# Attention followed by a top-1 mixture of experts: a new order for the last two batches, and evacuations and router steps on other engines

## The chip, the cores and the metric

The kernel runs on one core of a Trainium2 chip. The metric is device time in microseconds of one execution. The profile is one execution recorded by the hardware profiler; its span, from the first to the last instruction, is a little different from the measured times.

The engines have these names in the profile: PE is TensorE (PEld its weight loads), DVE is VectorE, ACT is ScalarE, POOL is GpSimd, SP is SyncE, which here only issues DMAs. Each engine runs its instructions in the order of the program, so an instruction that waits holds up all behind it on the same engine.

## The reference

Eight batches of 448 tokens, 12 heads of 64. Attention with a softmax whose denominator has an extra term, then a router by cosine similarity that picks one of eight experts for each token, and the two-layer expert, scaled by the router's probability.

```python
# q, k, v: (8, 12, 448, 64)
scores = scale * np.matmul(q, k.transpose(0, 1, 3, 2))
m = np.max(scores, axis=-1, keepdims=True)
e = np.exp(scores - m)
attn = e / (np.sum(e, axis=-1, keepdims=True) + np.exp(-m) + 1e-09)
x = np.matmul(attn, v)                      # -> (3584, 768) after the transpose

xn = x / (norm(x) + 1e-06)
en = expert_emb / (norm(expert_emb) + 1e-06)
logits = xn @ en.T / tau
expert_idx = np.argmax(logits, axis=1)
gate_w = softmax(logits)[expert_idx]
for e in range(8):
    mask = expert_idx == e
    h = np.maximum(x[mask] @ w1[e], 0.0)    # w1: (8, 768, 1024)
    out[mask] = gate_w[mask, None] * (h @ w2[e])   # w2: (8, 1024, 768)
```

The kernel computes, for each batch, the expert that most of its tokens chose; other experts follow in a conditional part at the end, which no token needs with these inputs.

## The kernel before

The program is a hand-written schedule. `put(slot, fn)` files a piece of work under a time mark, and at the end all pieces are emitted in the order of their marks. That gives each engine its order; waits between engines follow from the data and from the buffers. A slot has 8 marks (`NSLOT = 8`) and handles one pair of heads (48 pairs, `G`, six for each batch, `NP`). Attention runs through the slots; the expert work of a batch (15 products, `moe_chunks`) is spread over the slots of later pairs, from pair `LAG = 11` after the batch's first. `FILL` says where in each slot: three, three, one, two, three and three products.

```python
LAG = 2 * NP - 1
FILL = 2 * ((2.8, 5.3, 5.4),) + ((2.8,), (2.8, 5.4)) + 2 * ((2.8, 5.3, 5.4),)
```

Attention of one pair. `front_qk` transposes q and k; `scores` makes the scores in four parts (j = 0 to 3), exponentials on ScalarE and the subtraction of one on VectorE (`em`); `attend` multiplies by v in the next slot, takes the reciprocal of the denominator as exp(-ln) on ScalarE, and `normalise` makes x on VectorE. `square` gives the squares for the router's norms.

```python
def attend(k, g, s):
    ...
    def recip():
        nc.scalar.activation(rd[:], ps[:, :, 0:S], ACT.Ln, bias=1.0, scale=1.0 / (S + 1.0))   # L281
        nc.scalar.activation(rd[:], rd[:], ACT.Exp, scale=-1.0)                               # L282
    k.put(s + 0.04, rest)
    k.put(s + 2.3, recip)
```

The router of one batch: matmuls with the expert vectors (`router_mm`, L336) and a copy to SBUF (L342), transposes to token order (`router_tok`, L350), logits, maximum and one-hot (`router_logits`, L358 to L370), a matmul with ones that counts the choices (`router_pick`, L431), maximum and index of the counts (`router_count`), the index into a register (`router_index`), the loads of that expert's weights (`fetch`, L464), and on the side the probabilities (`router_pow`, `router_exp`, `router_act`, `router_gate`).

```python
def router_logits(k, b, tp):
    ...
    nc.vector.reduce_max(out=m[:], in_=l[:], axis=AX.X)
    nc.vector.tensor_tensor(out=l[:], in0=l[:], in1=m[:]..., op=ALU.subtract)      # L366
    nc.vector.tensor_scalar(out=oh[:], in0=l[:], ..., op0=ALU.is_equal)             # L368
    nc.vector.tensor_tensor(out=ohb[:], in0=oh[:], in1=k.mask[:], op=ALU.mult)      # L370

def router_exp(k, b):
    nc.gpsimd.tensor_scalar_add(nrm[:], nrm[:], 1e-6 * (S + 1.0))                   # L382
    nc.gpsimd.tensor_tensor(out=nrm[:], in0=nrm[:], in1=k.less[:], op=ALU.pow)      # L383
    nc.gpsimd.tensor_tensor(out=l[:], in0=l[:], in1=nrm[:]..., op=ALU.mult)         # L384

def router_act(k, b):
    k.nc.scalar.activation(l[:], l[:], ACT.Exp)                                     # L390
```

An expert product fills one PSUM buffer of the pool `work`, which has two, and is then evacuated to SBUF by ScalarE or VectorE, as the flag `vec` says. The pool is shared with the transposes of k, the fourth part of the scores and the router's transposes.

```python
n.work = pool("work", 2, space=PSUM)

def moe_h(k, xb, w1, f, hs, later=now, vec=False):      # 8 of them: first layer, L504
    ps = k.work.tile([128, 512], F32, name="work", tag="work")
    ...
        if vec: nc.vector.tensor_scalar_max(h[:], ps[:, 0:S], 0.0)                  # L512
        else:   nc.scalar.activation(h[:], ps[:, 0:S], ACT.Relu)                    # L514

def moe_y(...)     # 6: second layer, L532, evacuated at L522 (VectorE) or L524 (ScalarE)
def moe_yr(...)    # 1: the remainder of 64 tokens, L551, evacuated the same way
```

And the schedule:

```python
    put(-NSLOT, lambda: warm(k, 18))                      # 18 matmuls that only warm TensorE
    ...
    for b in range(B):
        s = ((b + 1) * NP + 1) * NSLOT
        put(s + 2.85, lambda b=b, s=s: router_mm(k, b, s + 2.75))
        put(s + 7.9, lambda b=b, s=s: router_tok(k, b, s + 7.9))
        s += NSLOT
        put(s + 0.16, lambda b=b: router_pick(k, b))
        put(s + 0.9, lambda b=b: router_pow(k, b))
        put(s + 6.9, lambda b=b: router_count(k, b))
        put(s + 7.05, lambda b=b: router_index(k, b))
        for i, o in enumerate((7.1, 10.5, 14, 20, 26, 32, 38)):
            put(s + o, lambda b=b, i=i: fetch(k, b, i))
        put(s + 7.2, lambda b=b: router_exp(k, b))
        put(s + 10.38, lambda b=b: router_act(k, b))
        ...
    late = {2.8: (4.7, False), 5.3: (7.3, True), 5.4: (8.5, True)}   # evacuation mark, VectorE?
    for b in range(B):
        pos = [((b * NP + LAG + i) * NSLOT, o) for i in range(NP) for o in FILL[i]]
        for (s, o), fn in zip(pos, moe_chunks(k, b), strict=True):
            put(s + o, lambda fn=fn, s=s, l=late[o]: fn(s + l[0], l[1]))
```

Of the kernel before, what the change touches and what calls it, by code (L numbers as in the profile page):

```python
# [23 lines left out]
SM = 384  # L24
# [112 lines left out]
def load_qk(k, n):  # L137

    nc = k.nc
    b, h0 = n // NG, n % NG * 2 * GP  # L140
    s = n % NG
    t = Net()
    t.qm = k.qkp.tile([128, 3, 2 * GP, DH], F32, name="qm", tag="qm")
    t.km = k.qkp.tile([128, 3, 2 * GP, DH], F32, name="km", tag="km")
    t.r, t.v = k.qkrest[s], k.vld[s]

    keng = nc.sync if n else nc.scalar
    for eng, dst, src in ((nc.sync, t.qm, k.q), (keng, t.km, k.k)):
        for j in range(3):
            eng.dma_start(  # L150
                dst[:, j, :, :], src[b, h0 : h0 + 2 * GP, 0:SM, :].rearrange("h (p t) d -> t p h d", t=3)[j]
            )
    for eng, h, src in ((nc.sync, 0, k.q), (keng, 1, k.k)):
        eng.dma_start(t.r[64 * h : 64 * h + 64, :, :], src[b, h0 : h0 + 2 * GP, SM:S, :].rearrange("h p d -> p h d"))
    k.ld[n] = t


# [150 lines left out]
def on_pool(g):  # L308
    return g < LAG - 1 and g % NP < NP - 1
# [14 lines left out]
def square_add(k, g):  # L324
    acc = k.xs[g - g % NP][1]
    k.nc.vector.tensor_tensor(out=acc[:], in0=acc[:], in1=k.xs[g][1][:], op=ALU.add)


def router_mm(k, b, s):

    nc = k.nc
    ps = k.big.tile([128, 512], F32, name="rmm", tag="big")
    for r in range(2):
        for q in range(4):
            x = k.xs[b * NP + 3 * r + q][0] if q < 3 else k.xs[b * NP + (NP - 1) * r][1]
            nc.tensor.matmul(  # L336
                ps[32 * q : 32 * q + 32, 0:S], lhsT=(k.en[:, 3 * r + q, :] if q < 3 else k.ones32[:]), rhs=x[:],
                start=(r == 0), stop=(r == 1),
            )
    for c in range(NP):  # L340
        k.xs.pop(b * NP + c)
    k.put(s + 1.9, lambda: nc.scalar.copy(out=k.rr[:, 0:S], in_=ps[:, 0:S]))  # L342


def router_tok(k, b, s):

    nc, p = k.nc, k.rp
    tp = k.work.tile([128, 4, 128], F32, name="tok", tag="work")
    for t in range(4):
        nc.tensor.transpose(tp[:, t, :], k.rr[:, 128 * t : 128 * t + 128], k.ident[:])  # L350
    k.put(s + 0.12, lambda: router_logits(k, b, tp))


def router_logits(k, b, tp):

    nc, p = k.nc, k.rp
    nrm = p.tile([128, 4], F32, name="nrm", tag="nrm")
    nc.vector.tensor_copy(out=nrm[:], in_=tp[:, :, 96])  # L358
    l = p.tile([128, 4, E], F32, name="l", tag="l")
    nc.vector.reduce_sum(  # L360
        out=l[:], in_=tp[:, :, 0:96].rearrange("p t (q r) -> p t r q", q=3)[:, :, 0:E, :], axis=AX.X
    )
    m = p.tile([128, 4], F32, name="m", tag="m")
    nc.vector.reduce_max(out=m[:], in_=l[:], axis=AX.X)

    nc.vector.tensor_tensor(out=l[:], in0=l[:], in1=m[:].unsqueeze(2).broadcast_to([128, 4, E]), op=ALU.subtract)  # L366
    oh = p.tile([128, 4, E], F32, name="oh", tag="oh")
    nc.vector.tensor_scalar(out=oh[:], in0=l[:], scalar1=0.0, scalar2=None, op0=ALU.is_equal)  # L368
    ohb = p.tile([128, 4, E], BF16, name="ohb", tag="ohb")
    nc.vector.tensor_tensor(out=ohb[:], in0=oh[:], in1=k.mask[:], op=ALU.mult)  # L370
    k.ohb[b], k.lg[b] = ohb, (l, nrm)


# [14 lines left out]
def router_act(k, b):  # L388
    l = k.lg[b]
    k.nc.scalar.activation(l[:], l[:], ACT.Exp)  # L390
# [44 lines left out]
def router_count(k, b):  # L435

    nc, p = k.nc, k.rp
    cnt = k.cnt_all[:, b, :]
    nc.vector.reduce_sum(out=cnt, in_=k.cp.pop(b).rearrange("p (t e) -> p e t", e=E), axis=AX.X)
    mx = p.tile([128, 8], F32, name="mx", tag="mx")  # L440
    k.mx[b] = mx[:, 0:1]
    nc.vector.max(mx[:], cnt)
    nc.vector.max_index(k.idx_all[:, b, :], mx[:], cnt)
    idf = p.tile([128, 1], F32, name="idf", tag="idf")
    nc.vector.tensor_copy(out=idf[:], in_=k.idx_all[:, b, 0:1])
    oh0 = k.oh0_all[:, b, :]
    nc.vector.tensor_scalar(out=oh0, in0=k.iota[:], scalar1=idf[:, 0:1], scalar2=None, op0=ALU.is_equal)


def router_index(k, b):  # L450
# [17 lines left out]
def fetch(k, b, i):  # L468
    w = w_piece(k, k.e0[b], i)
    k.wts[b][i // 3 > 0].append(w)  # L470
# [177 lines left out]
        nc.tensor.matmul(ps[:], lhsT=idb[:, 0:128], rhs=idb.unsqueeze(1).broadcast_to([128, 2, 256]), start=True, stop=True)  # L648


def pipeline(k):

    G = B * NP
# [2 lines left out]
    def put(slot, fn):  # L656
        at.setdefault(round(slot, 3), []).append(fn)
# [24 lines left out]
    for g in range(G):  # L682
        s = g * NSLOT
        put(s - NSLOT + 4.2, lambda g=g, s=s - NSLOT + 4.2: front_qk(k, g, s))
        put(s + 0.8, lambda g=g: front_v(k, g))
        rest = (3, 0.12, 2.3, 2.7) 
        for j, o, pa, pv in ((0, 0, 0.3, 1.5), (1, 0.05, 0.4, 2.6), (2, 5.2, 6, 7.7), rest):
            put(s + o, lambda g=g, j=j, pa=s + pa, pv=s + pv: scores(k, g, j, pa, pv))

        s += NSLOT  # L690
        put(s + 0.1, lambda g=g, s=s: attend(k, g, s + 0.1))
        put(s + 4.75, lambda g=g, s=s: normalise(k, g, s + 4.75))
        put(s + NSLOT + (4.68 if on_pool(g) else 2.35), lambda g=g: square(k, g))
        if 0 < g % NP < NP - 1:
            put(s + 2 * NSLOT + 0.6, lambda g=g: square_add(k, g))
    put(-NSLOT, lambda: warm(k, 18))
    for g in range(LAG):
        for o in (2.8, 5.4):
            put(g * NSLOT + o, lambda: warm(k, 3))
    for b in range(B):  # L700
        s = ((b + 1) * NP + 1) * NSLOT
        put(s + 2.85, lambda b=b, s=s: router_mm(k, b, s + 2.75))
        put(s + 7.9, lambda b=b, s=s: router_tok(k, b, s + 7.9))
        s += NSLOT
        put(s + 0.16, lambda b=b: router_pick(k, b))
        put(s + 0.9, lambda b=b: router_pow(k, b))
        put(s + 6.9, lambda b=b: router_count(k, b))
        put(s + 7.05, lambda b=b: router_index(k, b))
        for i, o in enumerate((7.1, 10.5, 14, 20, 26, 32, 38)):
            put(s + o, lambda b=b, i=i: fetch(k, b, i))  # L710
        put(s + 7.2, lambda b=b: router_exp(k, b))
        put(s + 10.38, lambda b=b: router_act(k, b))
        s += NSLOT
        put(s + 6.95, lambda b=b: keep_rows(k, b))
        put(s + 7.0, lambda b=b: keep_xb(k, b))
        put(s + 6, lambda b=b, s=s: router_gate(k, b, s + 6))

    late = {2.8: (4.7, False), 5.3: (7.3, True), 5.4: (8.5, True)}
    for b in range(B):
        pos = [((b * NP + LAG + i) * NSLOT, o) for i in range(NP) for o in FILL[i]]  # L720
        for (s, o), fn in zip(pos, moe_chunks(k, b), strict=True):
            put(s + o, lambda fn=fn, s=s, l=late[o]: fn(s + l[0], l[1]))
    while at:
        for fn in at.pop(min(at)):
            fn()
# [88 lines left out]
```

## Time and profile before

| | us |
|---|---|
| median of 3 runs | 440.58 (438.2 to 440.62) |
| span of the profiled execution | 444.5 |
| mean granted TensorE clock | 0.965 of full |
| PE, DVE, ACT, POOL busy | 394.7, 326.8, 296.7, 161.8 |
| expert weights, issue to landing | 8.4 (512 KB piece), 6.3 (384 KB piece) |

How to read the profile. Its first part gives the busy time of each engine with its share of the span and the number of instructions. A row of the waits says which engine and line waited for which, then us in total, how many times, and the longest. A row of the timeline gives the start in us, the length, engine, line, operation, what it writes and reads, and in square brackets how long the engine had stood idle before it and what ended that. A row by stretch gives for each engine its busy time in the stretch and the number of its instructions, and at the end the mean granted TensorE clock (1.00 is full), the DMA engines' busy share and the GB/s. Ends of matmuls are modelled, so the busy time of TensorE counts some waiting.

Three stages can be told apart in the busy time of slices: attention alone up to about 84 us, attention with expert work up to about 393 us, and the last router with the rest of the experts to the end.

### The profile page before, as it was taken

Reading aid. Unit: us, or ns where it says so; the run is one execution under the profiler, and the core shown is the slowest. Engines: PE = TensorE matmul, PEld = TensorE weight load, DVE = VectorE, ACT = ScalarE, POOL = GpSimd, SP = SyncE. Lnnn points to the kernel's source line nnn. Section 1 sums busy time; section 2 is a strip of 40 time slices with the busy share of each in tenths; the row PEclk is TensorE's granted clock in tenths of the full one; section 3 lists DMA queues with packets and bytes.
Section 4 is the critical chain, followed back from the end, with each engine's and each line's share of the span. In section 5 each row is a group of like instructions: output and inputs, shape, how many; then the busy total and the mean of one; then the engine's idle time right before and its main releaser. Section 6 shows DMA issues by size and latency. Waiting matters only on the chain.

```text
span 444.5 us, 7234 instructions
## 1 busy us (share of the span) xinstructions
PE 394.7 (89%) x2306; PEld 244.2 (55%) x2306; DVE 326.8 (74%) x787; ACT 296.7 (67%) x442; POOL 161.8 (36%) x237
## 2 busy tenths in 40 slices
PE   6998996999799997999799997999699997998595
PEld 2566554665556565565466564665456564644253
DVE  3789976997778797887788796887778696764122
ACT  1898885869658787688568775869657784842111
POOL 3141337722542138212643137312651218305400
PEclk9899999999999999999899998999989998999789
DMA  9886438983998849993998849993799409914953
GB/s 179 203 193 143 110 79 171 193 172 90 203 227 193 160 86 235 196 216 72 202 206 194 161 92 242 169 201 81 162 223 181 91 1 177 192 41 80 240 91 127
DMA packets 133305, 69.75 MB, mean 157 GB/s; under 512 B 99464, under 2 KB 127112, under 8 KB 133264
## 3 DMA queue, kind: packets, MB, share of 16 engines
q1 hardware_dynamic: 115024, 43.63, 39.5%
q0 software_dynamic: 16384, 25.17, 35.0%
q10 hardware_dynamic: 1856, 0.46, 0.5%
q8 instruction: 19, 0.31, 0.3%
q14 instruction: 22, 0.18, 0.1%
HBM read 83.39 MB, written 16.52 MB: 225 GB/s over the span
## 4 chain that ended last, share of the span: by engine, by line
PE 47%; ACT 19%; DVE 17%; issue 6%; DMA 5%; POOL 5%; SPq 0%; POOLq 0%; ACTq 0%; DVEq 0%
PE work L504 12%; PE work L532 9%; DVE x L295 5%; PE av L273 5%; ACT rd L281 5%; ACT e L240 5%; PE big L229 4%; PE work L235 3%; DVE em L248 3%; PE rmm L336 3%; PE work L551 3%; DMA w<-in_moe_w_dram 2%; DVE qt L200 2%; POOL nrm L383 2%; ACT rd L282 2%
## 5 line engine op out<-in xcount | busy, mean ns | idle before, releaser
L240 ACT ACTIVATE e<-big 128x896 f32<-128x896 f32 x144 | 127.0, 920 | 62.5 <-PE big L229 62.1
L504 PE MATMUL work<-xb,w 128*128 128x448 bf16 x384 | 82.3, 359 | 11.1 <-ACT h L514 5.3
L248 DVE TENSOR_SCALAR em<-e 128x896 fp32r<-128x896 f32 x144 | 86.9, 629 | 2.0 <-ACT e L240 1.5
L295 DVE SCALAR_TENSOR_TENSOR x<-av,rd 64x448 f32<-64x448 f32 x96 | 66.3, 691 | 20.3 <-ACT rd L282 18.4
L532 PE MATMUL work<-w,h 128*128 128x384 bf16 x384 | 73.4, 343 | 2.9 <-ACT y L524 2.1
L273 PE MATMUL av<-em,vab 128*128 128x448 f32 x288 | 67.7, 371 | 0.0
L229 PE MATMUL big<-qt,kt 64*128 64x448 f32 x288 | 58.9, 446 | 5.7 <-ACT kt L196 3.5
L200 DVE CAST qt<-tq 128x448 fp32r<-128x448 f32 x48 | 30.0, 624 | 43.4 <-PE tq L191 43.0
L504 PEld LDWEIGHTS <-w 128*128 128x128 bf16 x384 | 37.5, 103 | 44.0 <-issue 11.8
L273 PEld LDWEIGHTS av<-em,vab 128*128 128x128 f32 x288 | 54.2, 190 | 4.9 <-DVE em L248 0.6
L464 POOL DMA_DIRECT2D w<-in_moe_w_dram x56 | 45.2, 808 | 31.6 <-DVE em L248 20.7
L532 PEld LDWEIGHTS <-h 128*128 128x128 bf16 x384 | 38.6, 104 | 32.9 <-issue 13.2
L178 POOL TENSOR_TENSOR vs<-vs,vld 128x256 f32<-128x256 f32 x48 | 35.3, 736 | 52.3 <-issue 25.9
L281 ACT ACTIVATE rd<-av 128x896 f32<-128x896 f32 x48 | 44.2, 921 | 8.5 <-PE av L278 6.1
L178 POOL TENSOR_TENSOR vs<-vld 128x256 f32<-128x256 f32 x24 | 17.5, 728 | 88.4 <-PE av L278 69.5
L282 ACT ACTIVATE rd<-rd 128x896 f32<-128x896 f32 x48 | 45.7, 952 | 1.5
L229 PEld LDWEIGHTS big<-qt,kt 64*128 64x128 f32 x288 | 24.7, 186 | 34.7 <-issue 9.4
L522 DVE TENSOR_SCALAR y<-work,g 128x384 f32<-128x384 f32 x40 | 24.6, 616 | 24.4 <-PE work L532 14.9
L514 ACT ACTIVATE h<-work 128x448 bf16<-128x448 f32 x32 | 17.1, 534 | 20.2 <-PE work L504 20.2
L512 DVE TENSOR_SCALAR h<-work 128x448 bf16<-128x448 f32 x32 | 19.9, 623 | 13.1 <-PE work L504 12.1
L551 PE MATMUL work<-w,h 128*64 128x384 bf16 x128 | 14.4, 373 | 16.6 <-ACT y L524 16.6
L196 ACT CAST kt<-tk 128x384 fp32r<-128x384 f32 x48 | 22.6, 472 | 9.3 <-PE tk L189 9.2
(105 smaller groups left out, 545.2 us busy)
## 6 DMA issues: line engine op xcount, KB each, us to landing
w<-in_moe_w_dram POOLq DMA_DIRECT2D x24, 512.0 KB, 8.4
w<-in_moe_w_dram POOLq DMA_DIRECT2D x32, 384.0 KB, 6.3
qm<-in_q_dram SPq DMA_DIRECT2D x72, 128.0 KB, 2.9
vld<-in_v_dram SPq DMA_DIRECT2D x24, 384.0 KB, 3.8
out_dram<-y SPq DMA_DIRECT2D x48, 192.0 KB, 6.0
km<-in_k_dram SPq DMA_DIRECT2D x69, 128.0 KB, 4.0
qkrest<-in_q_dram SPq DMA_DIRECT2D x24, 64.0 KB, 4.1
vld<-in_v_dram SPq DMA_DIRECT2D x48, 32.0 KB, 3.8
```

Of the source, the lines that this page charges most:

```text
L178: k.behind(nc.gpsimd.tensor_tensor(out=vs[:], in0=(vs[:] if j > 1 else t.v[:, :, 0, :]), in1=t.v[:, :, j, :], op=ALU.add))
L200: nc.vector.tensor_copy(out=qt[:], in_=pq[:, 0:S])
L229: nc.tensor.matmul(ps[:, h, 0:S], lhsT=kt[64 * h : 64 * h + 64, 128 * j : 128 * j + 128], rhs=qt[64 * h : 64 * h + 64, :], start=True, sto ...
L240: nc.scalar.activation(e[:], ps[:, :, 0:S], ACT.Exp, scale=scale)
L248: k.last = nc.vector.tensor_scalar_sub(em[:], e[:], 1.0)
L273: nc.tensor.matmul(ps[:, h, 0:S], lhsT=va[:, j, h : h + 2, :], rhs=k.ems[g, j][:, h, :], start=False, stop=(j == 2),)
L281: nc.scalar.activation(rd[:], ps[:, :, 0:S], ACT.Ln, bias=1.0, scale=1.0 / (S + 1.0))
L282: nc.scalar.activation(rd[:], rd[:], ACT.Exp, scale=-1.0)
L295: nc.vector.scalar_tensor_tensor(out=x[r, :], in0=ps[r, h, 0:S], scalar=ps[r, 0, S : S + 1], in1=rd[o, h, :], op0=ALU.add, op1=ALU.mult,)
L464: k.nc.gpsimd.dma_start(w[:], src)
L504: nc.tensor.matmul(ps[:, 0:S], lhsT=w1[c // 2][:, c % 2, 128 * f : 128 * f + 128], rhs=xb[:, c, :], start=(c == 0), stop=(c == NP - 1),)
L532: nc.tensor.matmul(ps[:, 0:SM], lhsT=hs[f][:, 128 * t : 128 * t + 128], rhs=w2[f // 2][:, f % 2, SM * n : SM * n + SM], start=(f == 0), st ...
```

## The change

- The first pair of heads of the first batch is loaded alone and ahead of the second, q on SyncE's queue and k on ScalarE's, with the remainders on SyncE's; fewer warming matmuls stand before it (15, not 18).
- Three small steps of the router's one-hot and two steps of the chosen expert's one-hot (now `router_first`, behind the first weight fetch) go from VectorE to GpSimd.
- The router's exponential on ScalarE (`router_act`) and the gates (`router_gate`) come one slot later.
- Evacuations of expert products change engines: the first in a slot goes to VectorE, the second to ScalarE, the last of a two-product slot to ScalarE.
- Batches 6 and 7 have an order of their own (`last_batch`): three products of batch 6 before the last router's matmuls, two between its steps, the other ten of batch 6 and all of batch 7 after it. The last router starts one slot earlier, all its weight fetches are issued close together, the first three ahead of the powers, and the last squares are earlier.

It is meant to take waits off ScalarE and VectorE and to shorten the end, where the last router has little beside it.

```diff
-    keng = nc.sync if n else nc.scalar
-    for eng, dst, src in ((nc.sync, t.qm, k.q), (keng, t.km, k.k)):
-        for j in range(3):
-            eng.dma_start(dst[:, j, :, :], ...)
-    ...
+    if n:
+        ...   # as before, all on nc.sync
+    else:
+        for h in range(0, 2 * GP, 2):
+            for eng, dst, src in ((nc.sync, t.qm, k.q), (nc.scalar, t.km, k.k)):
+                for j in range(2):
+                    eng.dma_start(dst[:, :, h + j, :], src[0, h + j, 0:SM, :].rearrange("(p t) d -> p t d", t=3))
+            for j, src in ((0, k.q), (1, k.k)):
+                nc.sync.dma_start(t.r[64 * j : 64 * j + 64, h : h + 2, :], ...)
 ... (router_logits)
-    nc.vector.tensor_tensor(out=l[:], ..., op=ALU.subtract)
+    nc.gpsimd.tensor_tensor(out=l[:], ..., op=ALU.subtract)
-    nc.vector.tensor_scalar(out=oh[:], ..., op0=ALU.is_equal)
+    nc.gpsimd.tensor_scalar(out=oh[:], ..., op0=ALU.is_equal)
-    nc.vector.tensor_tensor(out=ohb[:], ..., op=ALU.mult)
+    nc.gpsimd.tensor_tensor(out=ohb[:], ..., op=ALU.mult)
 ... (router_count)
-    nc.vector.tensor_copy(out=idf[:], in_=k.idx_all[:, b, 0:1])
-    nc.vector.tensor_scalar(out=oh0, in0=k.iota[:], scalar1=idf[:, 0:1], ..., op0=ALU.is_equal)
+def router_first(k, b):
+    nc.gpsimd.tensor_copy(out=idf[:], in_=k.idx_all[:, b, 0:1])
+    nc.gpsimd.tensor_scalar(out=k.oh0_all[:, b, :], in0=k.iota[:], scalar1=idf[:, 0:1], ..., op0=ALU.is_equal)
 ...
+def last_batch(k, s):                       # s = G * NSLOT
+    b = B - 1
+    at = [s + o for o in (0.5, 1.0, 1.5, 5.5, 6.5)] + [s + 7.5 + 0.5 * i for i in range(25)]
+    out = {0: (s + 0.95, True), 1: (s + 2.5, False), 2: (s + 4.8, True), 3: (s + 5.9, True), 4: (s + 6.6, False)}
+    for i, fn in enumerate(moe_chunks(k, b - 1) + moe_chunks(k, b)):
+        put(at[i], lambda fn=fn, l=out.get(i, (at[i] + 0.45, i % 2 == 1)): fn(*l))
+    put(s + 5.0, lambda: router_mm(k, b, s + 5.2))
+    put(s + 6.0, lambda: router_tok(k, b, s + 6.12))
+    put(s + 7.0, lambda: router_pick(k, b))
+    put(s + 7.1, lambda: router_count(k, b))
+    put(s + 7.2, lambda: router_index(k, b))
+    for i in range(7):
+        put(s + (7.3 if i < 3 else 7.9), lambda i=i: fetch(k, b, i))
+    put(s + 7.4, lambda: router_first(k, b))
+    put(s + 7.5, lambda: router_pow(k, b))
+    put(s + 7.6, lambda: router_exp(k, b))
+    put(s + 9, lambda: router_act(k, b))
+    put(s + 9.1, lambda: router_gate(k, b, s + 9.1))
+    ...
 ... (pipeline)
-        put(s + NSLOT + (4.68 if on_pool(g) else 2.35), lambda g=g: square(k, g))
+        put(s + (4.9 if g == G - 1 else NSLOT + 4.68 if on_pool(g) else NSLOT + 2.35), lambda g=g: square(k, g))
-    put(-NSLOT, lambda: warm(k, 18))
+    put(-NSLOT, lambda: warm(k, 15))
 ...
+        if b == B - 1:
+            last_batch(k, G * NSLOT)
+            break
 ...
+        put(s + 7.15, lambda b=b: router_first(k, b))
         put(s + 7.2, lambda b=b: router_exp(k, b))
-        put(s + 10.38, lambda b=b: router_act(k, b))
         s += NSLOT
         ...
+        s += NSLOT
+        put(s + 2.38, lambda b=b: router_act(k, b))
         put(s + 6, lambda b=b, s=s: router_gate(k, b, s + 6))
-    late = {2.8: (4.7, False), 5.3: (7.3, True), 5.4: (8.5, True)}
-    for b in range(B):
+    late = {2.8: (4.6, True), 5.3: (7.0, False), 5.4: (8.5, True)}
+    for b in range(B - 2):
+        ...   # the second product of a two-product slot: (8.15, False)
```

The marks of the copy after the router's matmuls and of the logits are written in another place but keep their values for the first seven batches.

## The prediction

> **What bounds the kernel now.** I read the page's busy shares first, then the waits of TensorE, then those of ScalarE, then one stalled stretch in order of time, and last the busy time by stretch.
>
> ```profile
> PE 394.7 (89%) x2306; PEld 244.2 (55%) x2306; DVE 326.8 (74%) x787; ACT 296.7 (67%) x442; POOL 161.8 (36%) x237
> ```
>
> TensorE is the fullest engine, and an 89% that holds modelled ends leaves under 50 us of visible gaps. So the first question is who makes these gaps.
>
> ```profile
> PE work L551 <- ACT y L524: 16.6, 6, 3.7
> PE work L504 <- ACT h L514: 5.3, 11, 0.5
> PE work L504 <- DMA w<-in_moe_w_dram: 5.2, 2, 2.9
> PE work L532 <- ACT y L524: 2.1, 6, 0.4
> ```
>
> The columns are us in total, times, longest. Six waits of about 2.8 us, one for each batch whose experts run beside attention, are the largest item: the remainder matmuls (L551) want a PSUM buffer that ScalarE has not emptied (L524).
>
> ```profile
> ACT l L390 <- POOL l L384: 20.1, 8, 3.3
> ```
>
> ScalarE in turn stands in its queue before the router's exponential (L390) until GpSimd has finished the two powers and the product before it. It does so once a batch, 2.5 us on average. The timeline of batch 4's stall shows the three linked:
>
> ```profile
> 265.69 1.31 POOL L383 TENSOR_TENSOR nrm<-nrm,less 128x4 f32<-128x4 f32 x1
> ...
> 267.36 0.23 ACT L390 ACTIVATE l<-l 128x32 f32<-128x32 f32 x1 [2.34 <-POOL l L384]
> 267.50 0.90 ACT L281 ACTIVATE rd<-av 128x896 f32<-128x896 f32 x1
> ...
> 269.28 0.56 ACT L524 ACTIVATE y<-work,g 128x384 f32<-128x384 f32 x1
> ...
> 269.90 1.81 PE L551 MATMUL work<-w,h 128*64 128x384 bf16 x16 [2.79 <-ACT y L524]
> ...
> 271.63 2.74 PE L532 MATMUL work<-w,h 128*128 128x384 bf16 x8
> ```
>
> The power (1.31 us) holds L390; behind L390 stand the logarithm, its exponential and the copy L524; behind L524 stands TensorE. The last line matters as much: eight L532 matmuls take 2.74 us here, while sixteen take 2.76 us elsewhere. The stall also costs clock, as the stretches show (the figure after the brackets of POOL is the granted TensorE clock):
>
> ```profile
> 262.00:267.00 5.00, 5.00 (x32) 3.55 (x32) 4.84 (x16) 2.62 (x4) 2.78 (x3) 1.00 0.89 164
> 267.00:270.00 3.00, 0.21 (x4) 0.21 (x4) 0.98 (x4) 2.61 (x5) 2.47 (x6) 1.00 1.04 205
> 270.00:274.30 4.30, 4.30 (x24) 1.93 (x23) 2.44 (x8) 1.03 (x2) 3.64 (x6) 0.61 1.13 267
> 282.00:290.00 8.00, 7.53 (x46) 4.81 (x43) 6.73 (x15) 6.00 (x9) 2.13 (x3) 1.00 0.81 159
> ```
>
> TensorE idles in 267 to 270, and then works at a mean clock of 0.61 for 4.3 us; in an undisturbed stretch it is at 1.00. The last row also shows the next limits: VectorE is busy 6.73 of 8 us, ScalarE 6.00.
>
> [...] 0.61 after a gap of 2.8 us, and 0.50 for 4.5 us (420.0 to 424.5) after the gap in the tail. [...] the small GpSimd add of L382 takes 0.23 us in the median, but 0.71 us where it starts beside an `em` subtraction on VectorE. This bears on the steps moved to GpSimd. [...] On these 32-element tiles the choice is nearly free: 0.24 us (L384, GpSimd) against 0.19 (L366, VectorE).
>
> **The change part by part.**
>
> *Router exponential one slot later.* It moves eight marks of the schedule on, to where its input has long been there, so the wait is gone and 0.23 us of work stays. To size it I take the times between first attention matmuls (L264) around each of the six stalls: 12.0, 10.3, 12.5, 12.4, 13.4 and 12.4 us, 73.0 in sum. The next slot carries three second-layer products as well; it takes 8.14 us (274.82 to 282.96), 0.34 of it a wait for L524, so 7.8, and the remainder product adds about 0.1. Six times 7.9 is 47.4, so 25.6 us are removed: 16.6 of waits and about 9 of half clock. In batch 0 no expert work runs yet, but the slot from 66.82 to 75.75 takes 8.9 us and the next 7.3, against about 6.4 for its neighbours: some 3 us more. Sum: 28.5 us.
>
> *Evacuations on other engines.* In a slot with three products, the first is now emptied by VectorE instead of ScalarE, the second by ScalarE instead of VectorE. Before, the first stood behind ln and exp on ScalarE, and the second product waited 0.48 us for it (the L504 row above, 5.3 us, and most of the 2.1 us of L532). VectorE sits idle at that moment, waiting for the transposed q (0.96 to 0.99 us in the two slots I looked at), so it can take the 0.62 us copy. It pushes the qt copy and the normalisation back by about 0.1 to 0.5 us; the normalisation ends some 0.9 us before the next attention matmul needs it, so this is just hidden. TensorE's dense work in such a slot is 7.28 us against 7.77 now. VectorE has about 6.6 to 7.3 us of work in the same slot, so I don't count all of it: 5 us of the 7.4.
>
> *Small router steps on GpSimd.* VectorE loses five steps of 0.15 to 0.23 us, about 1 us a batch. But three of them (subtract, compare, mask) lie between the maximum and the counting matmul, which TensorE and the logarithm wait for in order. At present mask ends at 257.74 and that matmul starts at 257.90. On GpSimd the three take about 0.9 us undisturbed instead of 0.7, and VectorE runs copies and subtractions back to back just then[...]. I put the delay at 0.9 us in six batches: minus 5.5 us. The one-hot of the chosen expert moves behind the first fetch, off any path.
>
> *Last two batches.* Before, seven of batch 6's fifteen products run ahead of the last router's matmuls, and these start at 398.63 although their last input is there at 397.3. The slot before also carries three. Now three precede the router. Chain afterwards: the last j = 2 subtraction about 0.6 us earlier, L281 at about 392.4 instead of 393.36, square done at 396.5, last router matmul over at 396.9 instead of 400.4. Then a product is put before the transposes and one before the count (up to 0.7 us lost), GpSimd adds 0.3, so the first weight fetch is issued near 402.8 instead of 405.26. The three first-layer fetches follow at once, instead of at 408.15 and 409.13 with powers between them. The first-layer weights came in spaced 3.2 to 3.5 us (products resumed at 413.7, 416.5, 420.0), so the third should land near 416.5. Twelve products of batch 6, about 15 us, are left to cover this. One new wait: the powers now follow the fetches, so the exponential L390 is ready only near 409.2, and the evacuation of the first second-layer product stands behind it on ScalarE; TensorE loses about 3 us there, with weights still coming. Batch 7 then starts near 417 and needs 18.7 us warm (before: 20 us from 420.02, of which 2.2 were half clock). With the 4.45 us from the last matmul's end to the span's end this gives about 441 against 444.5: 3.5 us.
>
> *First pair alone.* Before, the last piece of k (64 KB, queued behind three pieces on ScalarE's queue, issued at 4.04) held the transposes until 9.19. Now the first pair's pieces, half the bytes, come first. The 15 warming matmuls end near 6.6, and the transposes could start near 7. Later loads share the same full queues (DMA share 1.02 over the first 12 us), so I count 2 us.
>
> Sum: 28.5 + 5 - 5.5 + 3.5 + 2 = 33.5. I take 1 us off for friction, as VectorE comes near to full, and predict 440.6 - 32.5 = 408.
>
> **Rivals.** First, the wait only changes its owner: with slots of 7.3 us VectorE (up to 7.3 us of work) becomes the bound, or the normalisation comes late for the next attention matmul, which already waits for it nine times (3.0 us in total). Against it: the stalled slots have 4.5 us of slack, so only the evacuation gain and a part of the first would go. Time about 416. Second, the counting matmul waits two microseconds or more for GpSimd[...]; then half of the gain of the exponential is given back in the slot before[...]. For it: L409 on GpSimd has a median of 0.56 us against 0.22 at best. Time about 420. Third, DMA becomes the bound: its share is 0.81 to 0.83 of 50 us a batch, which is 0.93 of 44.5 us. Against it: stretches at 1.04 to 1.13 pass without a wait of TensorE for data in the middle. It would add a few us, 412. Fourth, everything overlaps as planned, the count isn't delayed and the tail keeps its clock: 398.
>
> **Range and chances.** 398 to 420 runs from the fourth rival to the second. The 2% mark is 431.8; for it three quarters of the gain would have to be lost, although its largest term is a wait whose cause is taken away outright. Faster by over 2%: 0.95; within 2%: 0.04; slower: 0.01.
>
> **What would show it.** In the profile after: L551 waiting for ScalarE gone, and L390 waiting for GpSimd under 4 us in sum, mostly the tail's; first-attention-matmul spacing of about 7.9 us where it was 12.4; mean clock 0.98 or more. The period of a batch, from one router matmul to the next, falls from 50.3 us to about 45. A new row of the counting matmul or the logarithm waiting for GpSimd's mask, near 5 us. First scores near 8 instead of 10.42. I am wrong if L551's gap is filled by another releaser, if the clock stays at 0.965, or if the tail from the last router's matmuls to the end does not shrink below 44 us (it is 45.9).

## The result, and the profile after

| | before | after |
|---|---|---|
| median, us (4 runs each) | 440.6 (438.2 to 440.84) | 419.1 (416.94 to 420.24) |
| ratio, with 95% interval | | 0.9518 [0.9465, 0.9571] |
| span of the profiled execution, us | 444.5 | 415.3 |
| mean granted TensorE clock | 0.965 | 0.992 |

The change makes the kernel 4.8% faster, 21.5 us. The prediction was 408, with 398 to 420; the result lies at the upper edge of that range. The two profiled spans differ by more, 29.2 us: the execution of the kernel before that was profiled took 446.05 us, well above its median. This will matter below.

The busy shares of the kernel after, from its page:

```profile
PE 384.4 (93%) x2303; PEld 239.6 (58%) x2303; DVE 326.0 (78%) x751; ACT 299.9 (72%) x438; POOL 179.9 (43%) x277
```

TensorE is busy 10.3 us less in all, for the same matmuls but three warming ones: its clock was nearer to full (0.992 in the mean, 0.965 before). VectorE and ScalarE have the work they had, in a shorter span; GpSimd is busy 18 us more. Line numbers shift: L551 is now L562, L524 is L535, L390 is L397, L264 is L271, L281 is L288, L336 is L343. The longest waits of TensorE (us in total, times, longest):

```profile
PE av L271 <- DVE x L302: 6.9, 10, 3.5
PE av L438 <- POOL ohb L377: 6.3, 7, 0.9
PE big L236 <- DVE qt L207: 3.6, 1, 3.6
PE work L562 <- ACT y L535: 2.0, 1, 2.0
```

And the wait of ScalarE that was the target, once 20.1 us in eight times:

```profile
ACT l L397 <- POOL l L391: 4.4, 1, 4.4
```

The six waits of the remainder product beside attention, 16.6 us, are gone. One of 2.0 us is new, in the tail, where the exponential waits for GpSimd; the prediction had about 3 us for it. In their place stands the new wait that the prediction put near 5 us: the counting matmul waits 0.9 us for GpSimd's mask in each of seven batches, 6.3 us in sum. The slot in which batch 4's stall was, and the two after it, by stretch (the figure after the brackets of POOL is the granted clock):

```profile
251.44:259.41 7.97, 7.97 (x57) 5.44 (x58) 7.33 (x19) 6.17 (x9) 5.52 (x9) 1.00 0.96 197
259.41:267.13 7.72, 7.72 (x50) 5.22 (x48) 6.90 (x17) 6.26 (x10) 5.62 (x9) 1.00 1.12 251
267.13:274.39 7.26, 7.26 (x45) 4.63 (x42) 6.62 (x15) 6.11 (x9) 4.01 (x7) 1.00 1.10 203
```

The first row is the 12.4 us slot: now 7.97, with TensorE busy all the time and its clock at 1.00. VectorE is at 7.33 of 7.97 us there.

The steady part repeats to a few hundredths of a microsecond from batch to batch, so a change can be read from the six slots, start to start of the first attention matmul (the columns are worked out from the starts of L264 or L271 in the timelines):

| slot of a batch | before | after |
|---|---|---|
| three first-layer products (two slots) | 7.77 each | 7.23 each |
| one product and the router's matmuls | 7.98 | 7.98 |
| two products and the count | 6.57 | 7.67 |
| two second-layer products and the remainder | 10.3 to 13.4 | 7.97 |
| three second-layer products | 8.14 | 7.72 |

### The profile page after: what moved, and what is told of

It is laid out like the page before. It is cut to its first block, busy times and chain, and to the rows that moved or that the text cites. A ratio compares the mean times of both kernels' runs of the same rounds, so it can differ in the third digit from the quotient of the medians.

```text
span 415.3 us, 7247 instructions
## 1 busy us (share of the span) xinstructions
PE 384.4 (93%) x2303; PEld 239.6 (58%) x2303; DVE 326.0 (78%) x751; ACT 299.9 (72%) x438; POOL 179.9 (43%) x277
## 5 line engine op out<-in xcount | busy, mean ns | idle before, releaser
L255 DVE TENSOR_SCALAR em<-e 128x896 fp32r<-128x896 f32 x144 | 88.5, 640 | 1.3 <-ACT e L247 0.4
L515 PE MATMUL work<-xb,w 128*128 128x448 bf16 x384 | 79.6, 352 | 0.9 <-DMA w<-in_moe_w_dram 0.4
L280 PE MATMUL av<-em,vab 128*128 128x448 f32 x288 | 68.7, 375 | 0.7 <-DVE em L255 0.7
L543 PE MATMUL work<-w,h 128*128 128x384 bf16 x384 | 68.3, 326 | 0.1
L280 PEld LDWEIGHTS av<-em,vab 128*128 128x128 f32 x288 | 55.6, 194 | 5.4 <-DVE em L255 1.0
L475 POOL DMA_DIRECT2D w<-in_moe_w_dram x56 | 43.4, 774 | 35.1 <-DVE vab L223 30.0
L515 PEld LDWEIGHTS <-w 128*128 128x128 bf16 x384 | 36.1, 102 | 38.9 <-DVE em L255 5.8
L288 ACT ACTIVATE rd<-av 128x896 f32<-128x896 f32 x48 | 44.4, 925 | 18.7 <-PE av L438 9.7
L185 POOL TENSOR_TENSOR vs<-vs,vld 128x256 f32<-128x256 f32 x48 | 37.9, 791 | 30.8 <-issue 28.8
L523 DVE TENSOR_SCALAR h<-work 128x448 bf16<-128x448 f32 x45 | 28.1, 624 | 29.4 <-PE work L515 29.0
L543 PEld LDWEIGHTS <-h 128*128 128x128 bf16 x384 | 36.0, 100 | 26.2 <-issue 5.4
L207 DVE CAST qt<-tq 128x448 fp32r<-128x448 f32 x48 | 29.7, 618 | 21.3 <-PE tq L198 21.1
L533 DVE TENSOR_SCALAR y<-work,g 128x384 f32<-128x384 f32 x31 | 19.1, 617 | 17.8 <-PE work L543 10.9
L535 ACT ACTIVATE y<-work,g 128x384 f32<-128x384 f32 x25 | 14.5, 580 | 20.6 <-PE work L543 15.8
L203 ACT CAST kt<-tk 128x384 fp32r<-128x384 f32 x48 | 22.5, 469 | 9.0 <-PE tk L196 8.7
L249 ACT ACTIVATE e<-work 128x448 f32<-128x448 f32 x48 | 26.4, 550 | 1.6 <-DVE em L255 1.4
```

Source lines behind the costliest of these rows:

```text
L185: k.behind(nc.gpsimd.tensor_tensor(out=vs[:], in0=(vs[:] if j > 1 else t.v[:, :, 0, :]), in1=t.v[:, :, j, :], op=ALU.add))
L207: nc.vector.tensor_copy(out=qt[:], in_=pq[:, 0:S])
L255: k.last = nc.vector.tensor_scalar_sub(em[:], e[:], 1.0)
L280: nc.tensor.matmul(ps[:, h, 0:S], lhsT=va[:, j, h : h + 2, :], rhs=k.ems[g, j][:, h, :], start=False, stop=(j == 2),)
L475: k.nc.gpsimd.dma_start(w[:], src)
L515: nc.tensor.matmul(ps[:, 0:S], lhsT=w1[c // 2][:, c % 2, 128 * f : 128 * f + 128], rhs=xb[:, c, :], start=(c == 0), stop=(c == NP - 1),)
```

## The experiments

The runs were made on four chips, each with runs of the kernel before. The medians of the kernel before were 440.6, 450.3, 441.4 and 441.6 us on the four, those of the changed kernel 419.1 and 418.2 on two of them. So a difference of a microsecond between chips says nothing, and the kernel before, which varies more, is best compared within one chip. The first four runs below were made on the chip of the 450.3 us, where the changed kernel itself was not run.

**The kernel before again.** No edit.

> The kernel before, profiled once more. The profiled executions of the two kernels differ by 29.2 us in span, the medians of the timed runs by only 21.5. Theory: the half clock after a stall of 2.3 to 2.8 us falls into some executions and not into others, so this profile has fewer slow second-layer products behind the stalled remainder product (L532 x8 near 1.4 us instead of 2.7 in at least two of the six places), a mean clock above 0.97 and a span near 438. Rival: the clock falls behind every stall of 2.8 us, and the first profile was only slow elsewhere; then at least five of six places show about 2.7 us again and the span is 442 or more.

448.87 us, span 447.3, clock 0.966. The theory falls and the rival stands: behind all six stalls the products ran slowly again (the sixteen L551 in 2.06 to 2.77 us and the eight L532 in 1.55 to 2.54, where the first profile has 1.49 and 1.47 at one place with a granted clock of 1.00). The waits of TensorE in this second profile begin with

```profile
PE work L551 <- ACT y L524: 19.8, 6, 3.7
```

19.8 us where the first profile had 16.6: the same six waits are 3.2 us longer in an execution that is 2.8 us longer. The timeline of one of them shows what stretched:

```profile
164.97 2.43 POOL L464 DMA_DIRECT2D w<-in_moe_w_dram  x1 [3.41 <-DVE em L248]
167.48 0.22 POOL L382 TENSOR_SCALAR nrm<-nrm 128x4 f32<-128x4 f32 x1
167.78 1.04 POOL L383 TENSOR_TENSOR nrm<-nrm,less 128x4 f32<-128x4 f32 x1
...
169.17 0.23 ACT L390 ACTIVATE l<-l 128x32 f32<-128x32 f32 x1 [3.22 <-POOL l L384]
...
171.71 2.77 PE L551 MATMUL work<-w,h 128*64 128x384 bf16 x16 [3.66 <-ACT y L524]
```

In the same place of the first profile:

```profile
164.78 0.76 POOL L464 DMA_DIRECT2D w<-in_moe_w_dram  x1 [3.40 <-DVE em L248]
165.63 0.22 POOL L382 TENSOR_SCALAR nrm<-nrm 128x4 f32<-128x4 f32 x1
165.94 1.30 POOL L383 TENSOR_TENSOR nrm<-nrm,less 128x4 f32<-128x4 f32 x1
...
167.58 0.23 ACT L390 ACTIVATE l<-l 128x32 f32<-128x32 f32 x1 [1.81 <-POOL l L384]
...
170.12 1.49 PE L551 MATMUL work<-w,h 128*64 128x384 bf16 x16 [2.26 <-ACT y L524]
```

The issue of the first weight fetch stands on GpSimd ahead of the power that ScalarE waits for. It took 0.76 us in the first profile and 2.43 in the second, and the wait of TensorE was 2.26 and 3.66 us; the products behind it ran at full clock in the first (granted 1.00; 1.49 us for sixteen) and nearly twice as long in the second (2.77). The twelve stalls of the two profiles have three lengths only. Where the issue took 0.76 us and the add behind it (L382) 0.22, TensorE waited 2.3 us (three stalls); where the add took 0.71, 2.8 us (four); where the issue took 2.4, 3.7 us (five, one of them in the first profile). So two variable instructions on GpSimd set the length of the stall, and the clock loss comes on top (0.62 to 0.64 granted over the 24 matmuls behind five of the six stalls of the first profile). That fits the wide spread of the kernel before (438 to 453 us in all runs); that it makes up the whole spread is not shown.

**The router's exponential alone.**

```diff
 # in the kernel before
-        put(s + 10.38, lambda b=b: router_act(k, b))
         ...
         s += NSLOT            # now s as for router_gate
+        s += NSLOT
+        put(s + 2.38, lambda b=b: router_act(k, b))
         put(s + 6, lambda b=b, s=s: router_gate(k, b, s + 6))
```

> The kernel before with only the router's exponential and gates one slot later. Theory: this one wait is the bulk of the gain; the slots of about 12.3 us become 8, so the time falls by 18 to 23 us to about 420, as much as the whole change brings, because its other parts cancel (evacuations about +9, small steps about -8, start and end near 0). Rival: the wait needs the other parts too (ScalarE still stands before the evacuations), then it falls by less than 14 us and the products in question still wait for ScalarE over 1 us each.

421.7 us (420.7 to 423.6): ratio 0.9483 [0.9314, 0.9651] to the kernel before, so some 23 us less, with 15 to 31 as the interval. Five of the seven runs of the kernel before on this chip lay over 1.5% above its fastest (441.1 us) and are left out of that ratio; against their median of 450.3 us it would be 28.6. Against the medians of about 441 us on the other chips it is 19 to 20, so the gain is 19 to 23 us, as expected. The slots are 7.77, 7.77, 8.00, 6.57, 8.27 and 8.27 us. Of the 16.6 us of waits, this is left:

```profile
PE work L551 <- ACT y L524: 1.4, 6, 0.2
```

The rival falls: nothing else was needed to end the stall. This one move, of an operation of 0.23 us, brings nearly all of the change's gain; all the rest together brings another 3 us or so.

In batch 0, where no expert work stood beside the stall, little was gained: the slot of the stall fell from 8.93 to 5.86 us, but the next two grew from 7.34 and 7.50 to 8.31 and 8.97. Steps of VectorE take longer there, and TensorE waits for them. One such step in the kernel before:

```profile
75.85 0.25 DVE L479 SCALAR_TENSOR_TENSOR keep_i<-keep_f,row 128x1 uint32<-128x1 f32 x1
```

And here:

```profile
72.52 1.45 DVE L479 SCALAR_TENSOR_TENSOR keep_i<-keep_f,row 128x1 uint32<-128x1 f32 x1
73.00 0.95 POOL L318 TENSOR_TENSOR xs<-x 128x448 f32<-128x448 f32 x1
...
79.33 0.68 PE L229 MATMUL big<-qt,kt 64*128 64x448 f32 x4 [1.40 <-DVE kt L206]
```

GpSimd's square (L318) lies beside the long step; that it is the cause was not tried.

**The small steps back on VectorE.**

```diff
-    nc.gpsimd.tensor_tensor(out=l[:], ..., op=ALU.subtract)
+    nc.vector.tensor_tensor(out=l[:], ..., op=ALU.subtract)
     # and the same for the compare (oh) and the mask (ohb)
```

> The changed kernel with the three small steps (subtract, compare, mask) back on VectorE. Theory: the counting matmul then waits for nothing, the slot that holds it falls from 7.67 back to about 6.6 us in seven batches, and the time falls by 7 to 8 us to about 411.5. Rival: VectorE is so full now that the 0.7 us of steps a batch come back as waits for VectorE, and the time falls by less than 3 us.

415.75 us (415.71 to 416.56), 2.5 to 3.4 us under the changed kernel's two medians, which are of other chips: under half of what was expected. The slot with the count falls from 7.67 only to 7.05. The waits of TensorE say why:

```profile
PE av L271 <- DVE cnt_all L446: 3.3, 7, 0.6
```

With the mask in time, TensorE waits for VectorE's sum of the counts instead, which comes after the normalisation; and ahead of the normalisation stands the evacuation that the change put on VectorE. That this evacuation is the rest of it is tried below.

**The old start.** The loads of the first two pairs and the 18 warming matmuls of before, in the changed kernel (the diff of the change, reversed).

> The changed kernel with the loads of the first pairs and the 18 warming matmuls of before. Theory from the two traces: the new start wins 1.8 us up to the first scores and loses more later, as v is issued at 7.05 instead of 3.39 and VectorE's copy of v stands before the subtractions; with the old start the second attention slot falls from 7.2 to 5.7 us and the time falls by 1 to 2 us to about 417.5. Rival, the prediction: the new start is worth 2 us, so this is near 421.

419.5 us (415.56 to 420.34): no difference from the changed kernel's 419.1 and 418.2 that these runs can show, so neither the theory nor the rival is borne out. In the profile the second slot is back at 5.71 us and the attention matmuls of the fourteenth pair come at 104.4 us instead of 106.4, but this execution then lost 1.7 us in one slot to a late weight.

**The changed kernel again**, as the measure of the next three.

> The changed kernel again, on the same chip as the three that follow, so that they can be compared with it. 417 to 420 us; slots of 7.23, 7.23, 7.98, 7.67, 7.96 and 7.72 us in each batch, as in its first profile.

418.2 us (416.81 to 419.71), the slots as expected within two hundredths, but for two that are 0.1 and 0.6 us longer.

**The old evacuations.**

```diff
-    late = {2.8: (4.6, True), 5.3: (7.0, False), 5.4: (8.5, True)}
+    late = {2.8: (4.7, False), 5.3: (7.3, True), 5.4: (8.5, True)}
-    l=((8.15, False) if n == 2 and o > 5.3 else late[o])
+    l=late[o]
```

> The changed kernel with the evacuations on the engines and marks of before (first product of a slot on ScalarE, second on VectorE). Theory: each of the two first-layer slots goes back from 7.23 to 7.77, the two second-layer slots rise by 0.3 to 0.5, and the slot with the count falls by 0.5, since VectorE no longer copies there ahead of the normalisation: about 1.2 us a batch, so the time rises by 6 to 8 us. Rival, the prediction's own sum: 5 us or less.

431.3 us (427.66 to 432.46), 13.1 us above the changed kernel and more than the 6 to 8 of the theory; between the fastest runs of the two it is 10.9. The slots: 7.77, 7.77, 7.99, 7.60, 8.27 and 8.27, which is 47.7 a batch against 45.8. From the attention matmuls of the fourteenth pair to those of the forty-seventh it is 262.5 us against 253.2 in the run beside it, 9.3 us more. The slot with the count falls by 0.07 only, not 0.5. The waits for ScalarE are back:

```profile
PE work L515 <- ACT h L525: 4.8, 10, 0.5
...
PE work L562 <- ACT y L535: 3.7, 7, 2.0
PE work L543 <- ACT y L535: 2.8, 6, 0.5
```

Another 3.4 us of the profile came before that stretch, about half of it in the first two slots, and 3.1 us after it. Neither the first slots nor the tail are touched by the edit, so 9.3 us is the better measure of it. In the tail it was the clock, as far as the lengths of the matmuls show it (its mean is 0.980 in this profile and 0.992 in the run beside it): the same two waits as in the changed kernel (3.5 and 2.0 us) were followed by a longer time of slow matmuls. In the changed kernel's run beside it the three products after the last attention took 3.57 us, here 4.99; the 32 second-layer matmuls after the remainder took 5.37 and here 6.81.

**v ahead of the second pair.**

```diff
         for h in range(0, 2 * GP, 2):
             ...
+            if h == 0:
+                k.ld[n] = t
+                load_v(k, n)
```

> The changed kernel with v of the first two pairs loaded between the first pair and the second, instead of behind both. Theory: v was what the new start lacked; the first attention matmul comes near 14.6 us instead of 16.56, the second slot takes 5.8 instead of 7.2 as TensorE keeps its clock, and the time falls by about 3 us. Rival: the second pair of q and k is now late instead, and the time changes by less than 1 us.

415.7 us (414.72 to 416.46), 2.5 us under the changed kernel. The first attention matmul comes at 14.79 instead of 16.27, the second slot takes 5.71 instead of 7.23. So the loss at the start was v. The timeline of the changed kernel shows it on VectorE:

```profile
11.27 0.43 DVE L223 CAST vab<-vld 128x512 fp32r<-128x512 f32 x1 [2.50 <-DMA vld<-in_v_dram]
...
15.94 0.83 PE L236 MATMUL big<-qt,kt 64*128 64x448 f32 x4 [3.56 <-DVE qt L207]
...
17.61 2.42 PE L280 MATMUL av<-em,vab 128*128 128x448 f32 x6
```

The copy of v stands in VectorE's queue before the subtractions, waits 2.5 us for its load, and TensorE then stands 3.56 us and works on at half clock (0.53 granted from 17.61 to 20.00): six L280 matmuls take 2.42 us, and 1.37 with v loaded earlier.

**Steps on VectorE and the count slot's product on ScalarE.**

```diff
 # on top of the small steps back on VectorE; n is the number of products of the slot
-    l=((8.15, False) if n == 2 and o > 5.3 else late[o])
+    l=((8.15, False) if n == 2 and o > 5.3 else (4.7, False) if n == 2 else late[o])
```

> The changed kernel with the three small steps on VectorE and, in the slot that holds the count, the product's evacuation on ScalarE as before. With the steps alone moved back that slot fell only from 7.67 to 7.05, and TensorE then waited for VectorE's sum of the counts. Theory: the 0.62 us evacuation standing ahead of the normalisation is the rest of it; the slot falls to 6.6, and the time to about 412.5, 3 us under the version with the steps alone (415.75). Rival: VectorE is full in that slot whatever stands there, and the slot stays above 6.9.

412.5 us (411.57 to 413.73). The slot is at 6.57 in five batches and 6.82 in one. The theory holds. The slot in the four combinations: 7.67 us with the steps on GpSimd and the evacuation on VectorE (the changed kernel), 7.05 with both on VectorE, 7.60 with the steps on GpSimd and the evacuation on ScalarE, 6.57 with the steps on VectorE and the evacuation on ScalarE. Two waits lie side by side there, and taking one away shows little of what both cost.

**Both mends**, the last two edits in one kernel.

> The changed kernel with both mends that gained: the three small steps on VectorE with the count slot's product on ScalarE (412.5 alone) and v of the first pairs between the first pair and the second (415.7 alone, 418.2 without either). Theory: they touch different stages and add up, 410 us. Rival: VectorE is the bound over the whole length, and the second mend brings less than 1 us here: above 411.5.

409.1 us (408.17 to 409.18), 3.4 us under the version before it: they add up. One loss stays: in batch 0, in these and the later versions, the second of the slots named under the router's exponential takes 9.6 to 10.3 us, as TensorE waits 2.3 us for VectorE there and works on slowly (six L283 matmuls in 2.44 us, 1.37 in the slot before; at 76.40 in the first profile of the kernel before six such matmuls took 2.44 us at a granted clock of 0.50).

**A product in slot 47.** Line numbers are three higher in the versions with both mends: L280 is L283, L271 is L274, L515 is L518.

```diff
-    at = [s + o for o in (0.5, 1.0, 1.5, 5.5, 6.5)] + ...
-    out = {0: (s + 0.95, True), ...}
+    at = [s + o for o in (-5.2, 1.0, 1.5, 5.5, 6.5)] + ...
+    out = {0: (s - 3.4, True), ...}
```

> The version with both mends, and the first product of batch 6 moved from slot 48 into slot 47, where TensorE stands still for 3.5 us before the last attention matmuls and then runs those at half clock (six L280 matmuls 2.6 us instead of 1.4). Theory: the idle time falls to about 2.3 us, the clock stays up, the last router starts 1.2 us earlier and the time falls by 1 to 2 us. Rival: the clock falls all the same, or VectorE's evacuation delays the normalisation, and the time is within 0.5 us.

406.7 us (406.41 to 407.14), 2.4 us under the version without it, ratio to the kernel before 0.9197 [0.9135, 0.926]. This is the fastest version of the study. The last attention in the version without it, from its timeline:

```profile
356.59 0.74 PE L274 MATMUL av<-emx,vab 64*128 64x448 f32 x2 [3.49 <-DVE x L305]
357.27 2.61 PE L283 MATMUL av<-em,vab 128*128 128x448 f32 x6
```

And in this one:

```profile
356.04 0.47 PE L274 MATMUL av<-emx,vab 64*128 64x448 f32 x2 [2.34 <-DVE x L305]
356.44 1.64 PE L283 MATMUL av<-em,vab 128*128 128x448 f32 x6
```

The matmuls are nearly at full speed again (six in 1.64 us, 1.37 in the slot before). But the clock did not stay up altogether, though I had expected it (0.76 granted from 355 to 362 us): the next two products, twelve matmuls, took 3.84 us, and 24 such matmuls at full clock take 4.70. From the last attention to the router's matmuls it is 5.9 us instead of 7.7. The moved product is 1.2 us of that, so more of the gain comes from work put into idle time than from the clock.

**The last exponential later.** The edit is made in the version with both mends.

```diff
-    put(s + 9, lambda: router_act(k, b))
+    put(s + 10.47, lambda: router_act(k, b))
```

> The version with both mends, and the last router's exponential behind three evacuations on ScalarE instead of one, so that the remainder product (L562) of batch 6 doesn't wait for ScalarE. Theory: that 2.0 us wait covers nothing but the arrival of batch 7's weights; without it TensorE waits for the weights instead, from the same moment on, and the time stays within 0.7 us. Rival: the weights are there earlier, and the time falls by 1.5 to 2 us.

407.7 us (406.47 to 409.31) against 409.1: inconclusive, as the runs overlap, and the difference lies between what the theory and the rival said. In the profile the 1.9 us wait is gone; 0.7 us of it comes back as a wait for ScalarE two products later and 0.8 as a wait for the second-layer weights.

**The old end.** Batches 6 and 7, the last router, the last squares and sums as in the kernel before; the rest with both mends.

> The version with both mends, but batches 6 and 7 and the last router in the order of before. This sizes the new order of the end alone, for which the prediction had 3.5 us. Theory: 3 us, so the time rises by 2 to 4 us. Rival: with the waits of the middle gone the old order is as good, and it rises by less than 1 us; in the traces the stretch from the last first-attention matmul to the end was 53.2 and 51.9 us in two profiles of the kernel before and 50.5 in that of the changed one.

407.5 us (406.81 to 408.03) against 409.1 (408.17 to 409.18) with the new order. The new order of the end does not gain, it costs 1.5 us; neither theory nor rival had the old one ahead. With one product in slot 47 the new order (406.7) is level with the old one, so most of its cost is that gap. The last attention and the wait for weights of the version with the old end:

```profile
355.78 0.47 PE L274 MATMUL av<-emx,vab 64*128 64x448 f32 x2
356.19 1.49 PE L283 MATMUL av<-em,vab 128*128 128x448 f32 x6
357.65 4.70 PE L518 MATMUL work<-xb,w 128*128 128x448 bf16 x24
...
382.86 8.50 PE L518 MATMUL work<-xb,w 128*128 128x448 bf16 x44 [2.95 <-DMA w<-in_moe_w_dram]
```

Three products in slot 47 keep TensorE busy up to the last attention, and four more run at full speed before the router (granted clock 1.00 from 340 to 363 us). The first weights are asked for 13.2 us after the first line (369.01 in that profile), 15.1 us with the new order (371.70 after 356.59). The old end then waits 2.95 us for weights, but what follows stays at full speed (44 matmuls in 8.50 us, granted clock 0.99 from 384 to 405 us).

## Why the prediction came out as it did

The measured time lies in the range, 11 us above the point, and two of the four timed runs at its upper end (419.76 and 420.24). Three terms of the sum were too large (the stall by 6 to 9 us, the end by 5, the start by 2) and one too small (the evacuations, by about 4). That these leave it within the range is partly luck.

Its signs came near to what was said: the mean clock is 0.992, the period of a batch 45.8 us, L390's wait 4.4 us and all in the tail, the first scores at 8.64, and from the last router's matmuls to the end it is 43.7 us.

- *Router exponential, 28.5 us.* Mechanism right, size not: the stall ended with this move alone, but from profile to profile it shortened the span by 22.5 us (444.5 to 422.0), and between the medians of the timed runs by 19 to 23. In the profiles, 6 us of the 28.5 are missing. The six slots fell from 73.0 us to 49.7 in sum, 8.27 each and not 7.9, as the evacuations were still in the old places; the six slots behind them grew by 0.7 in sum; and batch 0 gave 0.6 instead of 3, since its next two slots took back what the first one gained. The other part is the base: the stall was read off an execution of 446.05 us and subtracted from a median of 440.6, although the length of this very stall changes from one execution to the next (2.3 to 3.7 us each).
- *Evacuations, 5 us.* Undersized: undoing them cost 13.1 us, and 9.3 us of the profile's difference lie in the steady part. I had taken 7.4 us of visible waits and cut them for VectorE's load. The cut was wrong: the first-layer slots did reach 7.23 us, under the 7.28 of dense work worked out. And the waits don't show all of it: the slot with the remainder gained too (8.27 to 7.97), which was hidden behind the stall.
- *Small steps on GpSimd, minus 5.5 us.* Right in size: the count waits 0.9 us in each batch, and the slot grew by 1.1. Undoing them alone gave 2.5 to 3.4 us, with the evacuation of that slot 5.7. The delay of 0.9 us in the prediction was my estimate; no run had shown it. From the start of the first step to the end of the third it is 0.97 us in the tail, where VectorE stands still for 1.39 us, and 1.80 in batch 0. The steps run longer beside work of VectorE: the compare on GpSimd takes 0.80 us in the median and 0.31 in the tail, the mask 0.50 and 0.25; in all seven batches the compare ends 0.06 to 0.07 us after the subtraction of VectorE (0.6 us) that runs beside it. What holds the steps up no run here shows. For the add of L382 an `em` subtraction alongside was not enough by itself: it took 0.71 us in three places of the first profile and 0.22 in two others (115.45 and 165.63), and in all five such a subtraction starts 0.06 us after it.
- *The end, 3.5 us.* Wrong: it costs 1.5 us, as measured in the version with both mends. I noted that slot 47 would carry no product and did not ask what TensorE does there. That slot is bound by the chain over ScalarE and VectorE (6.12 us before, 5.99 after, and 5.99 with three products in it), so TensorE stood 3.5 us instead of working and went into the last attention at half clock (0.50 granted over its six L280 matmuls), in some executions into the products behind it too (eighteen matmuls in 3.56 us in one, 4.99 in another). The prediction had read the loss of clock behind a stall of 2.8 us and did not use it on the gap that the change opens. So the chain was not shortened: the last router matmul was to end 3.5 us earlier and ended 0.3 us earlier, counted from the start of slot 47's attention (14.8 us after it, 15.1 before), and the first fetch, forecast 2.5 us earlier, came 0.5 later (20.6 us against 20.1). The sum had a slip besides: 417 + 18.7 + 4.45 is 440.2, not 441; and the products had resumed 2.8 and 3.5 us apart, not 3.2 to 3.5. The 2.7 us by which the tail is shorter in the first two profiles are mostly the old tail's half clock behind its waits for weights (2.2 us), which the version with the old end does not have in that place.
- *The start, 2 us.* Nothing came of it, and what the warming matmuls do for the clock no run shows: in the first profile it is 1.00 over the first 9 us. The first scores did come 1.8 us earlier (8.64 against 10.42), and the loads that this pushed back, v, were asked for at 7.05 instead of 3.39. I had looked at what the new order brings forward and not at who waits for what it moves back.

Of the rivals, the second (the count waits for GpSimd) was real, at half its size, so that its number, 420, is met by chance; the first was real in one slot only, the one with the count; DMA showed itself only in single late weights.

Worked out again with these sizes: 19 + 9.3 - 5.7 + 0 - 1.5 gives 21.1 us, and 21.5 were measured. The near agreement is partly luck: with 23 for the first term, or 13.1 for the second, it would be 25.

## What to carry to other kernels

An operation of 0.23 us in an in-order queue, waiting for a late input, made its slot 2 to 5 us longer here, some ten to twenty times its own length; move such an operation to where the input has long been there, before anything else is tuned. When a schedule is rearranged, ask of every product that is moved away what TensorE does in the time it leaves, and of every load that is brought forward what now lands later. And before a stall is subtracted from a median, check that the profiled execution took about that median, and whether the stall has the same length each time.

## What the runs showed of the hardware

- Gaps of TensorE of 2.3 to 3.7 us were followed by slow matmuls at eleven of the twelve stalls in the two profiles of the kernel before. In the first profile the granted clock over the 24 matmuls behind them was 0.62 to 0.64 at five stalls and 1.00 at the sixth. After 2.28 us in the second profile sixteen and eight matmuls took 2.06 and 2.54 us, after 2.26 us in the first 1.49 and 1.47. At some stalls the clock fell only after work had resumed: behind the gap of 2.79 us at 269.90 the first sixteen took 1.81 us (0.80 granted) and only the next eight the full 2.74 (0.50).
- A gap of about that length did not always cost the clock: behind one of 2.95 us in the tail (the version with the old end) 44 matmuls took 8.50 us, where behind one of 2.94 us in the kernel before, which followed close on another of 2.25, the same 44 took 10.71 (0.50 granted in their first 4.5 us).
- The issue of one and the same weight load on GpSimd took between 0.76 and 2.43 us in the same place of the program, and the small add behind it 0.22 or 0.71 us; nothing between was seen in the twelve stalls.
- ScalarE kept to the order of its queue: in batch 4 of the kernel before, the logarithm (L281), whose last matmuls (L278) had ended at 264.62, started at 267.50, behind the exponential that had stood waiting for 2.34 us.
